# Row and padding scatters one per step, beside a new order at the start: an FNet and mixture-of-experts kernel

## The chip, the core and the metric

The kernel runs on one core of a Trainium2 chip. TensorE (PE) multiplies matrices, VectorE (DVE) and ScalarE (ACT) work on tiles, GpSimd (POOL) issues the transfers whose addresses stand in a tile of indices (gathers and scatters), and SyncE (SP) issues the plain transfers. The metric is the device time of one execution in microseconds (us), lower is better. All data are float32.

## What is computed

Eight batches of 2496 rows by 256 columns get a two-dimensional Fourier transform, of which the real part is kept. The 19968 rows that come out go through a layer of eight experts: each row goes to the one with the largest logit.

```python
X = np.fft.fft(np.fft.fft(x, axis=1), axis=2).real        # x: (8, 2496, 256)
h = X.reshape(19968, 256)
logits = h @ w_gate                                       # (19968, 8)
idx = np.argmax(logits, axis=1)
gate = softmax(logits)[row, idx]
for e in range(8):
    y[idx == e] = np.maximum(h[idx == e] @ w1[e], 0) @ w2[e]   # 256 -> 1024 -> 256
out = gate[:, None] * y
```

## The kernel before

**Mixing, per batch.** `first(b)` is stage one, in 15 steps: for each of four quarters the rows are read by SP as `xl` and, mirrored, by a POOL gather (`xh`, L233); DVE folds the two (L241 to L252); PE multiplies with a constant (`s`), ACT copies the result (L266) and SP writes it to memory (`Td`, L297). `regroup` reads it back in another order (`t<-Td`, L307). `second(b)` is stage two, in two halves: a small product `pr`, copied into place by DVE (L318), then groups of two products `p` with an ACT copy `z` between (L328), which give `rows` (L334, L335) and logits. `route` (L349 to L377) takes the largest logit, the softmax, and, by matmuls `rk` against the one-hot choice, the place of each row among those of its expert; the result is `pi`, a table of 10 row numbers per partition. Ten scatters on POOL (`Xs<-rows,pi`, helper at L177) then put the half's rows, sorted by expert, into the memory area `Xs`. `route` yields after four and after eight of them.

**Plan.** `close(b)` works out, in some 18 small DVE operations (L400 to L426), which blocks of `Xs` are now full. For the last batch it first issues 16 padding scatters (`Xs<-pad,ti`, also at L177), which fill the ends of the experts' areas.

**Experts.** The blocks come in rounds: rounds 0 and 1 have small blocks (256 and 128 rows), round 2 three blocks of 512, rounds 3 to 6 five, round 7 five and then 21 of 256. For each block SP reads its number and expert out of the plan, then the rows (`xb`, L435) and the two weight matrices (`w_sb`, L438 and L440). PE transposes the rows (`pt`, L451; DVE copies them to `xT`, L452), multiplies with the first weights (`ph`), and ACT (L491) and DVE (L489) in turn write `hT` from two PSUM buffers; then `py`, which ACT scales into `y` (L503), and one POOL scatter per 128 rows writes `out_dram<-y,ro`. `y` has two buffers.

**The order.** It is written out by hand. Stage one and two of batch 0 come first, and from the sixth step of batch 0's stage two on, one step of batch 1's stage one goes beside each step. In the main loop the work of round b-1's expert blocks has `mixed(b)` at its side: three steps of batch b+1's stage one, then steps of batch b's stage two, every other one with a step of stage one beside it, then `close(b)`. `TICKS`, 42, says how many steps of the side are spread over 0.6 of the round's work. Each engine does its instructions in the order in which the program issues them, and POOL waits for the sources of each scatter before it takes the next.

The main loop, before:

```python
        total = 16 * sum(k * size for size, k, _ in rounds()[b - 1]) / BIG
        while done < total:
            w = next(work)
            done += w
            due += TICKS * w / (0.6 * total) if w else 1
            while due >= 1:
                next(side, None)
                due -= 1
```

Of the kernel before, what the change touches and what calls it, by code (L numbers as in the profile page):

```python
# [137 lines left out]
TICKS = 42  # L138
# [18 lines left out]
def kernel(ctx: ExitStack, tc, x, w_gate, w1, w2, out):  # L157
# [57 lines left out]
    con["tri"] = bp.tile([128, 128], F32, tag="y", name="tri")  # L215
# [12 lines left out]
    def load_x(b, q):  # L228
        xl = xp.tile([NA, 4, D], F32, tag="xl", name="xl", bufs=3)
        xh = xp.tile([NA, 4, D], F32, tag="xh", name="xh", bufs=3)  # L230
        src = x[b].rearrange("(p j) d -> p j d", j=NB)
        nc.sync.dma_start(out=xl[:], in_=src[:, 4 * q + 1:4 * q + 5])
        pool.indirect_dma_start(  # L233
            out=xh[:].rearrange("p j d -> p (j d)"), out_offset=None, in_=xrows,
            in_offset=bass.IndirectOffsetOnAxis(ap=ix[:, 4 * b + q:4 * b + q + 1], axis=0))
        return xl, xh
# [41 lines left out]
    def first(b):  # L278

        x0 = ahead.pop((b, "x0"))  # L280
        pm0 = xp.tile([NA, D], F32, tag="pm0", name="pm0")
        fold_d(pm0[:], x0[:], 1)
        for q in range(5):
            f = iter(())
            if q < 4:
                xl, xh = ahead.pop((b, q))
                f = fold(xl, xh, q)
            next(f, None)
            yield
            if q:  # L290
                t1 = xp.tile([NR, 4, D], F32, tag="t1", name="t1")
                half1(b, q - 1, 0, pm, pm0, t1)
            next(f, None)
            yield
            if q:
                half1(b, q - 1, 1, pm, pm0, t1)
                nc.sync.dma_start(out=Td[b][:, 4 * (q - 1) * D:4 * q * D], in_=t1[:].rearrange("p j d -> p (j d)"))  # L297
                load(b + (q + 2) // 4, (q + 2) % 4)
            next(f, None)
            pm = xh  # L300
            yield
# [10 lines left out]
    def second(b):  # L312

        for h in range(2):
# [3 lines left out]
            vec.tensor_copy(t4[:, :, H], pr[:])  # L318
# [22 lines left out]
    def route(b, h, rows, lg):  # L341
# [37 lines left out]
        for s in range(NSL):  # L379
            sent(put_row(Xs, pi[:, s:s + 1], rows[:, s], E * CAP - 1, "xs"), b)  # L380
            if s % 4 == 3:
                yield
# [7 lines left out]
    def plan(size, k, last):  # L390
# [3 lines left out]
        def one(name, *dims, dt=F32):  # L394
# [11 lines left out]
        vec.tensor_tensor(ex[:], ce[:], nb[:], op=ALU.subtract)  # L406
        vec.scalar_tensor_tensor(rb[:], ex[:], -float(size), gone[:], op0=ALU.mult, op1=ALU.add)
# [3 lines left out]
        vec.reduce_sum(ei[:], ge[:], axis=AX_X)  # L411
        vec.tensor_tensor(eq[:], bc(ei[:], 2, E + 1), bc(bk["e9"], 1, MOST), op=ALU.is_equal)
        vec.memset(val[:, :, E:E + 1], float(E * CAP))
        vec.scalar_tensor_tensor(val[:, :, 0:E], bc(bk["i"], 2, E), float(size), bc(rb[:], 1, MOST),
                                 op0=ALU.mult, op1=ALU.add)
        vec.tensor_tensor(val[:], val[:], eq[:], op=ALU.mult)
# [11 lines left out]
        return tab  # L428
# [26 lines left out]
    def experts(todo):  # L455
# [4 lines left out]
        for k, (b, size, last, at) in enumerate(todo):  # L460
            n, m = size // 128, BIG // size
            if not k:
                got = fetch(b, size, tabs[b, size, last], at)
# [34 lines left out]
            y = bp.tile([128, BIG // 128, D], F32, tag="y", name="y")  # L498
# [12 lines left out]
    def pads(b):  # L511
# [3 lines left out]
        for e in range(E):  # L515
            for k in range(2):
                sent(put_row(Xs, ti[:, e, k:k + 1], pad[:], ROWS - 1, "xs"), b)

    def close(b):

        if b == B - 1:
            pads(b)
        for size, k, last in rounds()[b]:
            tabs[b, size, last] = plan(size, k, last)
# [7 lines left out]
    def mixed(b):  # L532
# [9 lines left out]
        close(b)  # L542
        yield from one
# [5 lines left out]
    load(0, 2)  # L549
    const("m2", "ident", "rot", "rd", "rt")  # L550
# [3 lines left out]
    vec.memset(ones[:], 1.0)  # L554

# [16 lines left out]
    early = ahead_of(1)  # L572
    for k, _ in enumerate(second(0)):
        if k > 4:
            next(early, None)
    close(0)
    work = experts(todo)
    for b in range(1, B):

        side, done, due = mixed(b), 0, 0.0  # L580
        if b == 1:
            side = chain(early, side)
        total = 16 * sum(k * size for size, k, _ in rounds()[b - 1]) / BIG
        while done < total:
            w = next(work)
            done += w
            due += TICKS * w / (0.6 * total) if w else 1
# [3 lines left out]
        for _ in side:  # L591
            pass
    for _ in work:
        pass
# [24 lines left out]
```

## Time and profile before

| what | value |
|---|---|
| median of 3 runs | 1591.04 us (1586.5 to 1600.85) |
| profiled execution | 1588.63 us, span 1586.9 us |
| granted TensorE clock, mean | 0.961 |
| PE busy | 1453.8 us, 92% of the span |
| DVE, ACT, POOL busy | 25%, 18%, 24% |

The page's first part gives the busy time of each engine. The table of stretches cuts the span and gives for each piece the busy time of the engines, the clock that PE was granted (1.00 is full speed, 2.4 GHz; 0.5 is the lower level, 1.2 GHz) and the mean busy share of the DMA engines. In the order of time a row is one instruction or several alike in a row, with start, length, engine, line, operation, tiles, and in brackets how long the engine had stood idle before it and which engine or transfer released it; "issue" means that nothing in the profile held it, "remote" that the release came from something the trace does not name.

### The profile page before, as it was taken

To read this page: it belongs to the slowest core of one execution; us is meant where nothing else is said; L and a number is where in the kernel's file an instruction comes from. 1 tells how busy PE (TensorE), PEld (TensorE's weight loads), DVE (VectorE), ACT (ScalarE), POOL (GpSimd) and SP (SyncE) were. 2 spreads that over 40 slices of the span, in tenths; PEclk is the share of its full clock that TensorE was granted. 3 is DMA by queue.
4 is the path that set the end of the run, shared out by engine and by line. 5 is a ranking of instruction groups with operands and counts; after the bars stand their busy time and mean duration, and the time that the engine had idled before them with its cause. 6 is when DMAs were issued, how large, how long until landed. Compare 5 with 4: busy or idle time off the path is not lost.

```text
span 1586.9 us, 16900 instructions
## 1 busy us (share of the span) xinstructions
PE 1453.8 (92%) x6108; PEld 1076.8 (68%) x6108; DVE 393.3 (25%) x1154; ACT 279.8 (18%) x581; POOL 373.1 (24%) x382
## 2 busy tenths in 40 slices
PE   4668897988999899989999899969999999999998
PEld 2547776765776567656677567737676688888887
DVE  2454143233144113321143111321111111111111
ACT  1222121121122112211122112201111111111111
POOL 1334215133114211331114201361111011111111
PEclk9868999998999899999999999989999999999999
DMA  7365957635234442562233432342423345545551
GB/s 195 109 205 176 302 165 218 217 95 185 92 122 158 156 150 80 164 193 85 99 119 126 176 104 87 112 159 90 149 84 117 113 137 191 188 166 175 197 188 60
DMA packets 126132, 234.20 MB, mean 148 GB/s; under 512 B 12829, under 2 KB 85648, under 8 KB 126048
## 3 DMA queue, kind: packets, MB, share of 16 engines
q1 hardware_dynamic: 103491, 178.31, 34.1%
q0 software_dynamic: 20192, 53.43, 10.0%
q10 hardware_dynamic: 2365, 1.38, 0.4%
q8 instruction: 48, 0.79, 0.2%
q14 instruction: 36, 0.29, 0.1%
HBM read 179.15 MB, written 56.28 MB: 148 GB/s over the span
## 4 chain that ended last, share of the span: by engine, by line
PE 46%; issue 31%; POOL 5%; another core or an unknown queue 3%; DVE 1%; ACT 1%; POOLq 0%; DMA 0%; ACTq 0%; DVEq 0%
PE ph L162 19%; PE py L162 18%; PE p L162 5%; POOL out_dram L177 5%; PE s L162 2%; PE pt L451 1%; POOL Xs L177 1%; POOLq L177 0%; ACT hT L491 0%; DMA Xs<-rows,pi 0%; PE rk L162 0%; DVE xT L452 0%; ACT z L328 0%; ACT rows L334 0%
## 5 line engine op out<-in xcount | busy, mean ns | idle before, releaser
L162 PE MATMUL ph<-xT,w_sb 128*128 128x512 f32 (+2 forms) x1888 | 625.1, 485 | 42.3 <-issue 21.1
L162 PE MATMUL py<-w_sb,hT 128*128 128x256 f32 x2720 | 619.7, 382 | 4.5 <-DVE hT L489 3.3
L162 PEld LDWEIGHTS py<-w_sb,hT 128*128 128x128 f32 x2720 | 515.4, 192 | 83.7 <-issue 10.3
L162 PEld LDWEIGHTS ph<-xT,w_sb 128*128 128x128 f32 x1888 | 352.8, 194 | 265.3 <-issue 208.0
L177 POOL DMA_INDIRECT out_dram<-y,ro x170 | 165.7, 974 | 980.6 <-ACT y L503 931.2
L489 DVE TENSOR_SCALAR hT<-ph 128x512 f32<-128x512 f32 x170 | 117.5, 691 | 701.1 <-issue 354.4
L503 ACT ACTIVATE y<-py,xb 128x256 f32<-128x256 f32 x170 | 80.4, 473 | 636.3 <-PE py L162 588.1
L177 POOL DMA_INDIRECT Xs<-rows,pi x160 | 160.3, 1002 | 105.0 <-issue 48.8
L491 ACT ACTIVATE hT<-ph 128x512 f32<-128x512 f32 x170 | 101.5, 597 | 413.6 <-PE ph L162 356.2
L452 DVE COPY xT<-pt 128x512 f32<-128x512 f32 (+1 forms) x87 | 59.1, 679 | 258.0 <-PE pt L451 257.6
L162 PE MATMUL p<-rd,z 128*128 128x273 f32 x320 | 95.8, 426 | 19.1 <-DVE xl L252 7.1
L162 PE MATMUL s<-xh,w 78*80 78x256 f32 (+2 forms) x272 | 82.6, 435 | 26.9 <-DVE xh L243 14.1
L162 PEld LDWEIGHTS p<-rd,z 128*128 128x128 f32 x320 | 60.5, 206 | 33.2 <-issue 13.6
L162 PEld LDWEIGHTS s<-xh,w 78*80 78x80 f32 x272 | 45.5, 176 | 48.0 <-issue 16.7
L335 DVE COPY rows<-p 128x256 f32<-128x256 f32 x80 | 34.0, 425 | 152.4 <-ACT rows L334 121.2
L162 PEld LDWEIGHTS p<-m,t 128*128 128x128 f32 x320 | 50.5, 207 | 21.0 <-issue 18.8
L233 POOL DMA_INDIRECT xh<-in_x_dram,ix x32 | 31.3, 980 | 117.6 <-PE s L162 60.2
L162 PE MATMUL p<-m,t 128*128 128x128 f32 x320 | 52.1, 292 | 0.6 <-issue 0.6
L451 PE MATMUL pt<-ident,xb 128*128 128x128 f32 x340 | 51.6, 273 | 0.0
L451 PEld LDWEIGHTS pt<-ident,xb 128*128 128x128 f32 x340 | 42.9, 142 | 8.9 <-issue 0.2
L266 ACT COPY t<-s 80x512 f32<-80x512 f32 x64 | 37.0, 581 | 57.5 <-PE s L162 50.8
L328 ACT COPY z<-p 128x256 f32<-128x256 f32 x80 | 29.8, 373 | 83.0 <-PE p L162 67.9
(79 smaller groups left out, 317.8 us busy)
## 6 DMA issues: line engine op xcount, KB each, us to landing
w_sb<-in_moe_w_dram SPq DMA_DIRECT2D x118, 1024.0 KB
xb<-Xs SPq DMA_DIRECT2D x28, 516.0 KB
Td<-t SPq DMA_DIRECT2D x32, 320.0 KB
t<-Td SPq DMA_DIRECT2D x16, 640.0 KB
xl<-in_x_dram SPq DMA_DIRECT2D x32, 312.0 KB
xb<-Xs SPq DMA_DIRECT2D x27, 258.0 KB
out_dram<-y,ro POOLq DMA_INDIRECT x170
Xs<-rows,pi POOLq DMA_INDIRECT x160
```

The source lines that it names most:

```text
L162: nc.tensor.matmul(o, lhsT=lhsT, rhs=rhs, start=start, stop=stop)
L177: return unordered(pool.indirect_dma_start(out=dst, out_offset=bass.IndirectOffsetOnAxis(ap=idx, axis=0), in_=rows, in_offset=None, bounds ...
L233: pool.indirect_dma_start(out=xh[:].rearrange("p j d -> p (j d)"), out_offset=None, in_=xrows, in_offset=bass.IndirectOffsetOnAxis(ap=ix[: ...
L266: act.copy(t1[:, 2 * half:2 * half + 2], ps[:])
L328: act.copy(z[:], p2[:])
L335: vec.tensor_copy(rows[:, k + 1, 0:D], free(p3[:], D, [-1, D]))
L451: nc.tensor.transpose(pt[:, c, t], xb[:, 2 * h + t, c * 128:(c + 1) * 128], ident[:])
L452: vec.tensor_copy(xT[:, :, 256 * h:256 * h + 128 * n], pt[:].rearrange("p c t k -> p c (t k)"))
L489: vec.tensor_scalar(o, ph[:], 0.0, None, op0=ALU.max)
L491: act.activation(o, ph[:], ACTF.Relu)
L503: act.activation(y[:, i], py[:], ACTF.Copy, scale=xb[:, i, D + 1:D + 2])
```

## The change

Row scatters and padding scatters yield after each one and not after every fourth or never; the padding is no longer in `close` but goes one scatter per step beside the expert blocks that come after the last mixing. Output tiles `y` have three buffers. The plan is a generator in five pieces, and `close` is interleaved with the other steps (`woven`). The fourth quarter of x of batch 0 is loaded with the first three, into a tile of its own tag. The copy of `pr` goes from DVE to ACT. Seven steps of batch 1's stage one come before batch 0's stage two, and then one with every other step. The steps of the side are spread over 0.7 of the round (44 steps), and experts wait for the first plan by yielding. An activation with Exp runs at the start.

```diff
-TICKS = 42
+TICKS = 44
...
-    con["tri"] = bp.tile([128, 128], F32, tag="y", name="tri")
+    con["tri"] = bp.tile([128, 128], F32, tag="xT", name="tri", bufs=1)
...
     def load_x(b, q):
-        xl = xp.tile([NA, 4, D], F32, tag="xl", name="xl", bufs=3)
-        xh = xp.tile([NA, 4, D], F32, tag="xh", name="xh", bufs=3)
+        if (b, q) == (0, 3):
+            both = bp.tile([128, 8, D], F32, tag="w1", name="x03")
+            xl, xh = both[0:NA, 0:4], both[0:NA, 4:8]
+        else:
+            xl = xp.tile([NA, 4, D], F32, tag="xl", name="xl", bufs=3)
+            xh = xp.tile([NA, 4, D], F32, tag="xh", name="xh", bufs=3)
...
-                load(b + (q + 2) // 4, (q + 2) % 4)
+                if b or q > 1:
+                    load(b + (q + 2) // 4, (q + 2) % 4)
...
-            vec.tensor_copy(t4[:, :, H], pr[:])
+            act.copy(t4[:, :, H], pr[:])
...
             sent(put_row(Xs, pi[:, s:s + 1], rows[:, s], E * CAP - 1, "xs"), b)
-            if s % 4 == 3:
-                yield
+            yield
...
-    def plan(size, k, last):
+    def plan(b, size, k, last):
...
         vec.tensor_tensor(ex[:], ce[:], nb[:], op=ALU.subtract)
+        yield
...
-        return tab
+        yield
+        tabs[b, size, last] = tab
...
             if not k:
+                while todo[0][:3] not in tabs:
+                    yield 0
                 got = fetch(b, size, tabs[b, size, last], at)
...
-            y = bp.tile([128, BIG // 128, D], F32, tag="y", name="y")
+            y = bp.tile([128, BIG // 128, D], F32, tag="y", name="y", bufs=3)
...
                 sent(put_row(Xs, ti[:, e, k:k + 1], pad[:], ROWS - 1, "xs"), b)
+                yield
+
+    def woven(*parts):
+        parts = list(parts)
+        while parts:
+            for p in list(parts):
+                if next(p, p) is p:
+                    parts.remove(p)
+                else:
+                    yield
...
-        if b == B - 1:
-            pads(b)
         for size, k, last in rounds()[b]:
-            tabs[b, size, last] = plan(size, k, last)
+            yield from plan(b, size, k, last)
...
-        close(b)
-        yield from one
+        yield from woven(close(b), one)
...
     load(0, 2)
+    load(0, 3)
...
+    warm = cp.tile([1, 1], F32, name="warm")
+    vec.memset(warm[:], 0.0)
+    act.activation(warm[:], warm[:], ACTF.Exp)
...
     early = ahead_of(1)
+    for _ in range(7):
+        next(early)
     for k, _ in enumerate(second(0)):
-        if k > 4:
+        if k % 2 == 0:
             next(early, None)
-    close(0)
...
         if b == 1:
-            side = chain(early, side)
+            side = woven(close(0), chain(early, side))
...
-            due += TICKS * w / (0.6 * total) if w else 1
+            due += TICKS * w / (0.7 * total) if w else 1
...
+    rest = pads(B - 1)
     for _ in work:
-        pass
+        next(rest, None)
```

On POOL, a regular batch (batch 5): `Xs<-rows,pi` are row scatters, `out_dram<-y,ro` output scatters, `xh` gathers of the next batch's x; x10 means ten in a row. Before, both halves:

```order
L177 DMA out_dram<-y,ro 19968x256 x2
L177 DMA Xs<-rows,pi 162048x258 x10
L233 DMA xh<-in_x_dram,ix 78x1024 x2
L177 DMA out_dram<-y,ro 19968x256 x2
L177 DMA Xs<-rows,pi 162048x258 x4
L177 DMA out_dram<-y,ro 19968x256
L177 DMA Xs<-rows,pi 162048x258 x6
L233 DMA xh<-in_x_dram,ix 78x1024
```

After, the first half:

```order
L177 DMA out_dram<-y,ro 19968x256 x2
L177 DMA Xs<-rows,pi 162048x258 x3
L237 DMA xh<-in_x_dram,ix 78x1024
L177 DMA Xs<-rows,pi 162048x258 x3
L177 DMA out_dram<-y,ro 19968x256
L177 DMA Xs<-rows,pi 162048x258 x2
L177 DMA out_dram<-y,ro 19968x256
L177 DMA Xs<-rows,pi 162048x258
L237 DMA xh<-in_x_dram,ix 78x1024
L177 DMA out_dram<-y,ro 19968x256
L177 DMA Xs<-rows,pi 162048x258
L177 DMA out_dram<-y,ro 19968x256
```

The ten row scatters of the first half, one row before, now stand in rows of 3, 3, 2, 1 and 1 with gathers and outputs between. The second half, behind the rows shown, has 1, 2, 2 and 5 with one output between each, where it had 4, an output and 6.

On POOL at the end of the last batch; `Xs<-pad,ti` are the padding scatters. Before:

```order
L177 DMA out_dram<-y,ro 19968x256 x2
L177 DMA Xs<-rows,pi 162048x258 x4
L177 DMA out_dram<-y,ro 19968x256
L177 DMA Xs<-rows,pi 162048x258 x6
L177 DMA Xs<-pad,ti 162048x258 x16
L177 DMA out_dram<-y,ro 19968x256 x75
```

After:

```order
L177 DMA Xs<-rows,pi 162048x258 x5
L177 DMA out_dram<-y,ro 19968x256 x8
L177 DMA Xs<-pad,ti 162048x258 x8
L177 DMA out_dram<-y,ro 19968x256
L177 DMA Xs<-pad,ti 162048x258
L177 DMA out_dram<-y,ro 19968x256
L177 DMA Xs<-pad,ti 162048x258
L177 DMA out_dram<-y,ro 19968x256
L177 DMA Xs<-pad,ti 162048x258
L177 DMA out_dram<-y,ro 19968x256
L177 DMA Xs<-pad,ti 162048x258 x5
L177 DMA out_dram<-y,ro 19968x256 x58
```

The sixteen padding scatters, which followed the last row scatters at once, now come behind eight more outputs, eight in a row and then singly, with a last group of five.

On PE at the start: `s` is stage one, `pr` the first product of stage two, `p` its products, with the tile that they read behind the arrow. Before, the end of batch 0's stage one and the first of its stage two:

```order
L162 MATMUL s_210<-xh,w_87 80x127
L162 MATMUL pg<-wg,rt 128x8 x4
L162 MATMUL pr<-t_222,rot 128x5
L162 MATMUL p_242<-m_88,t_222 128x128 x2
L162 MATMUL p_247<-m_88,t_222 128x128 x2
L162 MATMUL p_252<-rd,z 128x273 x2
L162 MATMUL p_258<-m_88,t_222 128x128 x2
```

After, the same place:

```order
L162 MATMUL s_212<-x_121,w_87 80x127
L162 MATMUL pg<-wg,rt 128x8 x4
L162 MATMUL s_250<-xh,w_87 80x256 x2
L162 MATMUL s_258<-xh,w_87 80x256 x2
L162 MATMUL pr<-t_224,rot 128x5
L162 MATMUL s_272<-xh,w_87 80x256 x2
L162 MATMUL p_282<-m_88,t_224 128x128 x2
L162 MATMUL p_287<-m_88,t_224 128x128 x2
L162 MATMUL p_292<-rd,z 128x273 x2
L162 MATMUL s_298<-xh,w_87 80x256 x2
L162 MATMUL p_309<-m_88,t_224 128x128 x2
```

Four matmuls of batch 1's stage one now stand ahead of `pr`, and others between it and the products of stage two; before, batch 1's first came only behind the `rk` of the first half.

## Rows read from the trace of the kernel before

**Rows 1.** Page, part 1: busy time, share of span and instruction count per engine.

```profile
PE 1453.8 (92%) x6108; PEld 1076.8 (68%) x6108; DVE 393.3 (25%) x1154; ACT 279.8 (18%) x581; POOL 373.1 (24%) x382
```

**Rows 2.** Table of stretches: from:to, length, busy time per engine, clock, DMA share, GB/s.

```profile
0.00:114.00 114.00, 61.40 (x241) 46.26 (x242) 49.48 (x174) 22.70 (x50) 34.16 (x36) 0.84 0.58 165
114.00:175.00 61.00, 52.56 (x247) 42.23 (x247) 21.64 (x85) 11.97 (x27) 26.49 (x27) 0.86 0.69 217
175.00:400.00 225.00, 196.10 (x936) 152.88 (x935) 73.90 (x241) 44.64 (x98) 65.44 (x67) 0.93 0.58 188
400.00:735.00 335.00, 318.89 (x1255) 217.33 (x1255) 88.53 (x261) 63.41 (x134) 84.10 (x87) 0.96 0.40 133
735.00:905.00 170.00, 164.58 (x659) 112.81 (x658) 46.39 (x134) 32.95 (x69) 39.36 (x41) 0.99 0.38 128
905.00:1080.00 175.00, 160.61 (x621) 107.69 (x620) 40.09 (x129) 28.77 (x62) 53.92 (x56) 0.97 0.34 117
1080.00:1580.00 500.00, 499.70 (x2159) 397.64 (x2157) 73.25 (x130) 75.18 (x141) 68.66 (x71) 1.00 0.43 147
```

**Rows 3.** Order of time, start: start, length, engine, line, instruction, idle before and releaser.

```profile
28.42 1.97 PE L162 MATMUL s<-xh,w 78*80 78x256 f32 x4 [2.06 <-issue]
...
43.25 0.56 PE L162 MATMUL pr<-t,rot 128*128 128x5 f32 x2 [8.79 <-DMA t<-Td]
...
60.75 0.17 DVE L375 TENSOR_TENSOR pi<-pf,far 128x10 int32<-128x10 f32 x1
...
62.12 0.43 PE L162 MATMUL pr<-t,rot 128*128 128x5 f32 x2
...
78.60 2.16 PE L162 MATMUL p<-rd,z 128*128 128x273 f32 x4 [6.61 <-DVE xl L252]
...
88.19 0.17 DVE L375 TENSOR_TENSOR pi<-pf,far 128x10 int32<-128x10 f32 x1
...
91.10 1.08 POOL L177 DMA_INDIRECT Xs<-rows,pi  x1 [0.30 <-issue]
...
107.22 0.38 SPq L435 DMA_DIRECT2D xb<-Xs  x1
...
107.80 0.39 SPq L438 DMA_DIRECT2D w_sb<-in_moe_w_dram  x1
...
113.76 1.53 PE L162 MATMUL ph<-xT,w_sb 128*128 128x256 f32 x6 [1.03 <-DMA w_sb<-in_moe_w_dram]
```

**Rows 4.** Order of time, padding scatters of the last batch.

```profile
1045.76 1.98 PE L162 MATMUL ph<-xT,w_sb 128*128 128x512 f32 x4 [1.38 <-issue]
...
1052.05 0.60 ACT L491 ACTIVATE hT<-ph 128x512 f32<-128x512 f32 x1 [11.43 <-remote]
...
1052.70 3.52 PE L162 MATMUL ph<-xT,w_sb 128*128 128x512 f32 x4 [4.96 <-issue]
...
1061.93 3.78 PE L162 MATMUL ph<-xT,w_sb 128*128 128x512 f32 x4 [5.71 <-issue]
```

**Rows 5.** Order of time, second half of batch 5, TensorE, ScalarE and GpSimd.

```profile
689.73 0.97 POOL L177 DMA_INDIRECT Xs<-rows,pi  x1 [1.75 <-DVE p_nb L400]
...
695.94 3.60 PE L162 MATMUL ph<-xT,w_sb 128*128 128x512 f32 x8
...
704.66 0.60 ACT L491 ACTIVATE hT<-ph 128x512 f32<-128x512 f32 x1 [3.84 <-remote]
...
705.32 5.63 PE L162 MATMUL ph<-xT,w_sb 128*128 128x512 f32 x6 [5.78 <-issue]
```

**Rows 6.** Order of time, an expert block with no mixing beside it.

```profile
1087.49 0.60 ACT L491 ACTIVATE hT<-ph 128x512 f32<-128x512 f32 x1 [2.79 <-PE ph L162]
```

**Rows 7.** Groups by line: busy, mean ns, idle before and releasers; the scatters.

```profile
L177 POOL DMA_INDIRECT out_dram<-y,ro x170 | 165.7, 974 | 980.6 <-ACT y L503 931.2 <-ACT lg L361 20.8 <-DVE ro L479 20.2
...
L177 POOL DMA_INDIRECT Xs<-rows,pi x160 | 160.3, 1002 | 105.0 <-issue 48.8 <-ACT t L266 27.6 <-ACT hT L491 10.2
...
L177 POOL DMA_INDIRECT Xs<-pad,ti x16 | 15.6, 973 | 4.9 <-issue 4.9
```

More of the change, by code (lines that the diff above doesn't have):

```diff
@@ L517, in pads @@
                 sent(put_row(Xs, ti[:, e, k:k + 1], pad[:], ROWS - 1, "xs"), b)
+                yield
+    def woven(*parts):
[5 more added lines that the diff above has]
+                else:
+                    yield
     def close(b):
-        if b == B - 1:
-            pads(b)
         for size, k, last in rounds()[b]:
-            tabs[b, size, last] = plan(size, k, last)
+            yield from plan(b, size, k, last)
     def ahead_of(b):
```

## The prediction

> **What bounds it now.** I read the profile page first, then the table of stretches, then the order of time where a stretch loses. The page [rows 1] says TensorE (PE) is busy 1453.8 of 1586.9 us. So the kernel is bound by PE, and what can be won is PE's idle time and the time that it works at a lower granted clock. The table [rows 2] says where these lie. In each row I take length minus PE busy as idle, and length times (1 - PEclk) as what the clock costs (an upper figure, since some low clock falls into idle time). The last 500 us lose 0.3 us: expert blocks alone run without a gap. The start (0 to 114) loses 52.6 us idle and 18.2 by the clock; 114 to 175 loses 8.4 and 8.5; 175 to 400, with the mixing of batches 2 and 3 beside expert blocks, 28.9 and 15.8; 400 to 735 (batches 4 and 5) 16.1 and 13.4; 735 to 905 (batch 6) 5.4 and 1.7; 905 to 1080 (batch 7 and the padding) 14.4 and 5.2. After 114 that is 73.2 us idle and at most 44.6 by the clock, about 118 in all, and it lies only where mixing runs beside experts.
>
> Why does PE wait there? In the order of time at the padding [rows 4], PE ends four `ph` matmuls at 1045.76 + 1.98 = 1047.74, but the ACT copy that only needs these starts at 1052.05, 11.43 us idle, released by "remote", and PE then stands 4.96 us. The same happens again (PE idle 5.71 before 1061.93). In a regular batch [rows 5] scatters start back to back from 689.73; PE ends `ph` at 695.94 + 3.60 = 699.54, ACT starts only at 704.66 and PE loses 5.78 us. Where no scatters run in a row the same copy starts on PE's end [rows 6]: idle 2.79, released by PE itself. So the suspect is neither ACT nor VectorE (DVE) but **the run of scatters on GpSimd (POOL)**: while POOL issues one every 1.28 us (0.97 busy and 0.30 between, [rows 7]), PE's message "done" reaches ACT and DVE up to 5 us late, `hT` is late, the two PSUM buffers of `ph` stay full, and PE stands; afterwards its clock is low for a while. The 170 output scatters, which wait for ACT (931.2 us of idle, [rows 7]), come one by one and in the last 500 us hold nothing up.
>
> **The change, part by part.** *One scatter per step.* It removes no instruction: 160 row scatters at 1002 ns, 16 padding ones at 973 and 170 output ones at 974 remain. Only the order on POOL moves. Before, a regular batch queues 10 row scatters in a row for its first half, and 4, an output, 6 and a gather for its second. After, it is 3, gather, 3, output, 2, output, 1 ... for the first, and 1, 2, 2, 5 with single outputs between for the second. What is spread by gathers and outputs that have to wait is spread in time too. But POOL does not wait for steps: outputs that are already due run at once. The row index of the second half comes about when the `py` part of a block ends, so its 10 scatters and 3 outputs may still take 13 x 1.28 = 16.6 us nearly without a break. I therefore let the first half's losses go and about half of the second's stay. Per stretch, against the idle plus clock worked out above: 400 to 735, 29.5, of which 40% = 12; 735 to 905, 7.1, of which 2; 175 to 400, 44.6, of which 12, because batch 2 keeps runs of 6 and 8 on POOL; 114 to 175, 16.9, of which 3 (that stretch is packed with transfers anyhow, DMA share 0.69). The shares are choices; their bounds are nothing, and all of it.
>
> *Padding moved behind the last plan.* Before, 16 pads follow the last 6 row scatters, and the two waits shown [rows 4] fall into them. After, the first 8 come while `ph` of the next block runs, the rest stand singly or behind outputs. Of 19.6 us I take 11. Eight in a row take 10.2 us, so a wait may remain there.
>
> *The start.* The chain [rows 3] goes: first matmul on the regrouped data (`pr`) of batch 0 at 43.25; `pi` of the first half at 60.75, 17.5 later; `pr` of the second half at 62.12, 1.4 later; `pi` of the second half at 88.19, 26.1 later, in which PE stands 6.61 for VectorE's fold of the x of batch 1, whose gather sat behind scatters, and does some 7 us of batch 1's stage one; first row scatter after that at 91.10, behind a gather; block read `xb` issued at 107.22, weights at 107.80, first `ph` at 113.76. After: x quarter 3 of batch 0 is read at the start and not after quarter 1; before, PE stood 2.06 us for it at 28.42, and the earlier read adds traffic to busy queues: between 0 and 3, I take 1.5, `pr` at 41.7. Seven steps of batch 1 fill the wait for the regrouped data, which is a wait for a transfer, so they delay nothing; `pi` at 41.7 + 17 = 58.7. The rest of stage one of batch 1 comes in the first half, where PE waited for the argmax anyway. `pr` of the second half at 60.4, and with no stage one in it and no wait on the fold 26.1 - 6.6 - 7 = 12.5 to 17 later; I take 15.8, `pi` at 76.2. No gather stands ahead, so 10 x 1.28 = 12.8 gives the last scatter ended at 89.2; `xb` some 2 later at 91.5, and the `ph` 6.5 after that (as 113.76 - 107.22) at 98. The matmuls ahead of it are the same, so 113.76 - 98 = 15.8 is won. The waits before it leave PE longer in low clock; I take off 2.8 and keep **13** (6 to 18: the lower end if the scatters still wait for a gather, the upper without the clock).
>
> *At nothing:* the copy of `pr` goes to ACT (16 small copies; ACT is busy 18% of the span [rows 1]); a third output buffer (nothing in these stretches waits for `y`; it only covers output scatters that stand behind a row scatter, 1.28 us; the last stretch has some 71 scatters in 500 us on POOL [rows 2], four to a block, so a block takes 28 us); the plan in five pieces, which delays DVE's other work less; the `tri` tile moved to a buffer not used before the first block. If cover were gone, an output scatter would be late by a run, some 10 us, and ACT would then wait for `y`. The early activation brings ACT's table load no earlier, since it still stands behind the constant loads that ACT issues. The side work now spreads over 0.7 of a round instead of 0.6; 0.3 of five 28 us blocks is 43 us before the next round needs its rows, so no fetch is late. Only round three, with three blocks, has 25, and may lose 0 to 3.
>
> **Sum.** 13 + 3 + 12 + 12 + 2 + 11 = 53. The profiled execution took 1588.6, so 1535.6; the median is 2.4 above it, so **1538** against 1591.
>
> **Rivals.** *All runs harmless.* If gaps of a few us between scatters are enough, the idle after 175 (64.8) goes whole and 13 at the start: 1591 - 78 = 1513. For it: the waits lie only in long runs. Against: the second half's 13.
>
> *Short runs harm as well.* If what counts is that POOL issues for ten or more us with or without outputs between, only the start and the padding are won: 13 + 11 = 24, so 1567. For it: [rows 5] shows the wait in a run that already had outputs in it.
>
> *POOL's runs are innocent.* Then the late "remote" releases have another cause that the change does not touch, and only the start counts: 1591 - 13 = 1578. Against it: DVE and ACT rows of the same shape lose nothing in the last 500 us, and the longest loss is where the longest run is. The Trainium skill, SBUF — State Buffer, section "Who interferes with whom", speaks for this one: DMA never contends with a compute engine, and PE and ACT never wait on anyone. By that rule spreading scatters frees nothing on PE. The trace does not agree in full: ACT waited 11.43 us for a PE that had ended [rows 4], although the port cannot be the reason; the rule covers ports, and the late signal may go another way, so I give it a small chance.
>
> *Slower.* Each scatter, alone too, holds PE's message back once, and 176 of them spread now hit 176 different handoffs instead of a few. It costs as much as is won at (118 + 13)/176 = 0.74 us each. At a scatter's own 0.98 us it is 172 - 131 = 41 slower, 1632. Against it: single output scatters in the last 500 us cost PE nothing [rows 2].
>
> **Chances.** Mine 0.54, all harmless 0.17, short runs harm 0.17, innocent 0.07, slower 0.05. The range reaches from the first to the third rival and a little over: 1512 to 1572; the likeliest case's own is 1525 to 1552. About 1% (16 us) is what a measurement of this kernel can tell: 1575 or less is faster, which the first three cases give, so 0.88; within it 0.07; slower 0.05.
>
> **What would show it.** First `ph` near 98; `pi` of batch 0's second half near 76 with no wait on the fold. Between 905 and 1080 PE idle about 6 instead of 14, and no "remote" wait of ACT over 5 us; between 400 and 735 idle near 8. POOL's rows no longer ten in a row at 1.28 us in a first half. Wrong: "remote" waits of the same length behind two or three scatters (short runs harm), or the waits gone altogether (harmless), or PE waits in the last 500 us beside single pads (slower).

## The result and the profile after

The changed kernel took 1534.05 us (median of 4 runs, 1528.0 to 1538.13), the kernel before 1595.9 (4 runs, 1586.5 to 1600.85) in the same measurement: a ratio of 0.9616, interval 0.9553 to 0.9679. On another chip it was 1527.35 against 1584.43, 0.9651 (0.9617 to 0.9684). The forecast was 1538, 53 us won; by the medians it is 61.9 here and 57.1 there.

The groups of runs went to different chips, and these are of two kinds: on two of them (and where the case was measured) the kernel before takes 1584 to 1600 us, on two others 1496 to 1497. Every ratio below is against the kernel before on the same chip. Two single runs far above the others of their kernel, 3054 us of the padding variant and 1904 us of the variant without the early read, enter no ratio.

The page of the changed kernel, part 1 (busy time, share of the span, instructions), answers to [rows 1]:

```profile
PE 1444.5 (94%) x6108; PEld 1073.5 (70%) x6108; DVE 390.3 (25%) x1139; ACT 283.7 (18%) x598; POOL 378.5 (25%) x382
```

With the spans, 1586.9 before and 1533.6 after, the 53.3 us won are 44.0 us less idle on PE (133.1 to 89.1) and 9.3 less busy time (1453.8 to 1444.5, the same matmuls at a mean clock of 0.973 and not 0.961). The table of stretches of the changed kernel answers to [rows 2]; columns as there:

```profile
0.00:114.00 114.00, 68.86 (x244) 48.71 (x244) 50.47 (x182) 23.55 (x55) 34.99 (x36) 0.85 0.61 165
114.00:175.00 61.00, 54.22 (x268) 44.82 (x268) 17.82 (x65) 12.38 (x28) 24.76 (x25) 0.89 0.77 226
175.00:400.00 225.00, 199.84 (x944) 155.89 (x945) 72.99 (x237) 46.46 (x104) 69.87 (x70) 0.95 0.58 186
400.00:735.00 335.00, 332.04 (x1326) 226.95 (x1325) 94.22 (x274) 67.91 (x144) 89.56 (x89) 0.99 0.44 142
735.00:905.00 170.00, 168.97 (x674) 115.13 (x673) 46.87 (x133) 34.55 (x73) 40.55 (x41) 1.00 0.41 136
905.00:1080.00 175.00, 173.94 (x689) 119.06 (x688) 43.02 (x133) 31.44 (x68) 40.36 (x42) 1.00 0.33 113
```

PE idle (length minus the second figure behind it), before and after: 52.6 and 45.1 in the first stretch, 8.4 and 6.8, 28.9 and 25.2, then 16.1 and 3.0, 5.4 and 1.0, 14.4 and 1.1. After 400 us nearly all the idle is gone, 30.9 of 35.9 us, and before that only 12.8 of 89.9.

Idle alone does not say what was won, since less idle can also mean slower work. A better count takes, at each border, the matmuls that are done by then, each at the time that its kind takes at full clock, and asks how far the changed kernel is ahead (an estimate from the matmul rows of both traces): 1 us at 114, 4 at 175, 10 at 400, 30 at 735, 35 at 905, 53 at 1080. On the other chip it is 1, 2, 7, 26, 33 and 52. So four fifths of the gain fall behind 400 us, and next to nothing into the start.

In the order of time of the changed kernel, the second half of batch 5 answers to [rows 5]:

```profile
702.31 7.03 PE L162 MATMUL ph<-xT,w_sb 128*128 128x512 f32 x16
...
704.28 0.60 ACT L501 ACTIVATE hT<-ph 128x512 f32<-128x512 f32 x1 [1.30 <-PE ph L162]
...
712.40 1.98 PE L162 MATMUL ph<-xT,w_sb 128*128 128x512 f32 x4 [0.93 <-issue]
713.12 0.60 ACT L501 ACTIVATE hT<-ph 128x512 f32<-128x512 f32 x1 [3.67 <-remote]
```

The late "remote" release is still there, 3.67, but PE now loses 0.93 where it lost 5.78. The start answers to [rows 3]:

```profile
24.75 1.28 ACT L575 ACT_TABLE_LOAD   x1 [24.75 <-DMA far<-c_far]
26.15 1.51 ACT L270 COPY t<-s 80x512 f32<-80x512 f32 x3
26.76 5.41 PE L162 MATMUL s<-xh,w 78*80 78x256 f32 x12 [6.58 <-ACT t L270]
...
45.49 0.59 PE L162 MATMUL pr<-t,rot 128*128 128x5 f32 x2 [0.45 <-DMA t<-Td]
...
55.64 2.01 PE L162 MATMUL p<-rd,z 128*128 128x273 f32 x8
...
67.39 0.43 PE L162 MATMUL pr<-t,rot 128*128 128x5 f32 x2
...
78.69 0.37 ACT L333 COPY z<-p 128x256 f32<-128x256 f32 x1 [3.21 <-remote]
79.11 1.12 PE L162 MATMUL p<-m,t 128*128 128x128 f32 x4 [4.21 <-issue]
...
80.03 3.32 PE L162 MATMUL p<-rd,z 128*128 128x273 f32 x8
...
87.80 0.17 DVE L380 TENSOR_TENSOR pi<-pf,far 128x10 int32<-128x10 f32 x1
...
106.46 0.21 SPq L443 DMA_DIRECT2D xb<-Xs  x1
...
115.17 5.32 PE L162 MATMUL ph<-xT,w_sb 128*128 128x256 f32 x12 [3.45 <-DVE xl L253]
```

Nothing of the forecast of the start came about as told: the first `ph` is at 115.17, not 98, and no earlier than in the kernel before (113.76). PE stands 7.5 us less there, but it has hardly done more: 244 matmuls against 241 in the first stretch, where the difference is four more of the products `p` and one `ph` less. It was busy 68.86 us for them against 61.40. Some 3 of these 7.5 us are a lower clock during the work (by the granted clock over PE's busy time an estimated 13.7 us are lost to it, against 10.4): the eight `p` at 80.03, behind a late `z`, take 3.32 us at a mean granted clock of 0.67 (80 to 84 us), the eight at 55.64 take 2.01 at 1.00 (54 to 58 us). What makes up the rest, no row settles.

### The profile page after: what moved, and what is told of

It is laid out like the page before. It is cut to its first block, busy times and chain, and to the rows that moved or that the text cites. A ratio compares the mean times of both kernels' runs of the same rounds, so it can differ in the third digit from the quotient of the medians.

```text
span 1533.6 us, 16870 instructions
## 1 busy us (share of the span) xinstructions
PE 1444.5 (94%) x6108; PEld 1073.5 (70%) x6108; DVE 390.3 (25%) x1139; ACT 283.7 (18%) x598; POOL 378.5 (25%) x382
## 4 chain that ended last, share of the span: by engine, by line
PE 49%; issue 30%; POOL 6%; DVE 1%; another core or an unknown queue 0%; POOLq 0%; ACT 0%; ACTq 0%
PE py L162 20%; PE ph L162 20%; PE p L162 5%; POOL out_dram L177 4%; PE s L162 3%; POOL Xs L177 1%; PE pt L459 1%; POOLq L177 0%; PE rk L162 0%; DVE hT L499 0%; ACT hT L501 0%; DVE xT L460 0%; PE pr L162 0%; DVE rows L340 0%
## 5 line engine op out<-in xcount | busy, mean ns | idle before, releaser
L162 PE MATMUL ph<-xT,w_sb 128*128 128x512 f32 (+2 forms) x1888 | 615.1, 479 | 18.2 <-issue 6.4
L177 POOL DMA_INDIRECT Xs<-rows,pi x160 | 165.2, 1032 | 105.8 <-issue 54.7
L162 PE MATMUL s<-xh,w 78*80 78x256 f32 (+2 forms) x262 | 78.8, 431 | 26.5 <-DVE xh L247 18.2
L237 POOL DMA_INDIRECT xh<-in_x_dram,ix x31 | 30.9, 995 | 143.8 <-PE s L162 124.9
L339 ACT COPY rows<-p 128x256 f32<-128x256 f32 x80 | 29.8, 373 | 57.9 <-PE p L162 55.5
```

The lines of the kernel that those rows point to most:

```text
L162: nc.tensor.matmul(o, lhsT=lhsT, rhs=rhs, start=start, stop=stop)
L177: return unordered(pool.indirect_dma_start(out=dst, out_offset=bass.IndirectOffsetOnAxis(ap=idx, axis=0), in_=rows, in_offset=None, bounds ...
L237: pool.indirect_dma_start(out=xh[:].rearrange("p j d -> p (j d)"), out_offset=None, in_=xrows, in_offset=bass.IndirectOffsetOnAxis(ap=ix[: ...
L339: act.copy(rows[:, k, 0:D], p3[:, 0:D])
```

## The experiments

### The two kernels on another chip

> The changed kernel itself again, since the kernel before took 1496 us in the four comparisons made first and 1591 when the case was measured. Two theories. One: the late messages belong to the chip or its hour, not to the program; where the kernel before takes 1496 the scatters have nothing to give, only the start is won, and the ratio is 0.993 to 0.995; where it takes 1591 the ratio is 0.96 again. Two: the late messages belong to the program and something in the three variants happened to remove them; then the ratio is near 0.96 wherever it runs.

Measured: 0.9651 (0.9617 to 0.9684), the kernel before at 1584.43. On such a chip both theories give this ratio, so it does not decide between them. What does is that the kernel before itself takes 1496 us in some comparisons and 1584 or 1600 in others, and that two variants that had 0.994 and 0.995 on a chip at 1496 have 0.967 and 0.965 on one at 1600 (below). So the late messages come with the chip, or with the hour at which it was used: each chip was seen in one comparison only.

> The kernel before, for a trace from the same chip as the others of this call. If the late messages belong to the chip, PE idle between 400 and 1080 is either about 36 us (time near 1591) or under 5 (time near 1496), with the same runs of ten scatters at 1.28 us in both.

Measured: 1579.52, PE idle after 400 like that of [rows 2]:

```profile
400.00:735.00 335.00, 319.48 (x1253) 215.29 (x1252) 89.88 (x264) 65.02 (x136) 84.47 (x85) 0.97 0.42 140
735.00:905.00 170.00, 164.74 (x660) 113.06 (x659) 46.20 (x134) 32.83 (x69) 40.09 (x41) 0.99 0.37 126
905.00:1080.00 175.00, 160.87 (x624) 108.28 (x623) 39.38 (x128) 28.77 (x62) 54.52 (x56) 0.95 0.33 114
```

15.5, 5.3 and 14.1: 34.9 us, in the same runs of scatters.

### A run of scatters by itself

```diff
+            kind, count = PROBE.get(len(todo) - k, ("", 0))
+            for r in range(count):
+                if kind == "plain":
+                    nc.sync.dma_start(out=Jk2[128 * r:128 * r + 128], in_=pad[:])
+                    continue
+                put_row(Junk, (jt if kind == "put" else jo)[:, ...], pad[:], ..., "junk")
```

> The changed kernel with extra transfers at the start of six of the last blocks, where nothing else is mixed in: runs of 4, 8 and 12 scatters to a memory area that nobody reads, 12 scatters whose row numbers are all out of range (issued, nothing moved), 12 plain writes of the same size issued by SP, and 8 scatters again. If a run of scatters on POOL holds PE's messages back, PE waits none or little at 4, 1 to 3 us at 8, 5 or more at 12, and at the 12 that move nothing as well if it is the issuing, not if it is the data; none at the plain writes. If the runs are innocent, PE waits nowhere. On a chip on which the kernel before takes 1496 I expect no wait at any of them.

Measured, on the chip of the two runs above, as PE idle in gaps over 0.5 us between the first scatter of a run and 6 us after its last:

| put at the start of a block | in a row | PE idle |
|---|---|---|
| scatters | 4 | 0 |
| scatters | 8 | 0.76, and 0 the second time |
| scatters | 12 | 1.45 and 2.27 |
| scatters with all rows out of range | 12 | 2.18 |
| plain writes by SP | 12 | 0 |

The run of 12 scatters, in order of time:

```profile
1324.75 0.60 PE L459 MATMUL pt<-ident,xb 128*128 128x128 f32 x4
...
1329.50 0.69 DVE L460 COPY xT<-pt 128x512 f32<-128x512 f32 x1 [7.32 <-PE py L162]
...
1330.25 3.72 PE L162 MATMUL ph<-xT,w_sb 128*128 128x256 f32 x16 [1.45 <-DVE xT L460]
...
1336.24 3.72 PE L162 MATMUL ph<-xT,w_sb 128*128 128x256 f32 x16 [2.27 <-ACT hT L513]
```

The transposes `pt` end at 1325.35; the copy that needs them, and for which the rows show nothing else to wait for, starts at 1329.50, 4.15 later. Around the 12 that move nothing it is the same (`jo` is their table of rows):

```profile
1391.49 0.69 DVE L460 COPY xT<-pt 128x512 f32<-128x512 f32 x1 [8.05 <-issue]
1391.95 0.97 POOL L177 DMA_INDIRECT Junk<-pad,jo  x1 [0.30 <-issue]
...
1392.24 2.23 PE L162 MATMUL ph<-xT,w_sb 128*128 128x256 f32 x7 [2.18 <-DVE xT L460]
```

So on this chip it is POOL's run itself that delays PE's messages, with no mixing and no plan beside it; not the data moved, and not a transfer of that size as such. This is one execution, with one run of each kind and two of eight. In it the wait begins at about eight in a row and is smaller than I had put it (3.7 us for twelve, not five or more).

### Many short runs

```diff
                 put_row(out, ro[:, i:i + 1], y[:, i], NT - 1, "out")
+                for _ in range(2 if last else 0):
+                    put_row(Junk, jt[:, spent[0]:spent[0] + 1], pad[:], 96 * 128 - 1, "junk")
+                    spent[0] += 1
```

> The changed kernel with 84 extra scatters to an area that nobody reads, two behind each output scatter of the last 21 blocks, so never more than three in a row. The rival by which each scatter holds PE back once, 0.74 us or more, makes it 60 us slower than the changed kernel. By the prediction's own theory, three in a row cost nothing: the same within 3 us.

Measured, on the same chip: 1524.43 (1523.09 to 1525.78) against the changed kernel's 1527.35. 84 more scatters in runs of three cost nothing. The rival that ends slower, 0.74 us each, would have been 62 us slower; it is excluded for scatters in threes beside expert blocks.

### Row scatters ten in a row again

```diff
         for s in range(NSL):
-            sent(put_row(Xs, pi[:, s:s + 1], rows[:, s], E * CAP - 1, "xs"), b)
+            for r in range(4 * s, min(4 * s + 4, NSL)):
+                sent(put_row(Xs, pi[:, r:r + 1], rows[:, r], E * CAP - 1, "xs"), b)
             yield
```

All ten steps stay; only the scatters move together, into the order that the kernel before has on POOL.

> The changed kernel with the row scatters in three steps again (4, 4 and 2), all ten steps of each half kept, so that only their place on GpSimd's queue moves: ten in a row in a first half, four, an output and six in a second. Theory of the prediction (a run of scatters holds back PE's messages): the idle of PE between 400 and 905, 4.0 us in the changed kernel, goes back to some 15 to 21, the remote waits of ACT and DVE return, and the time is 20 to 30 us above the changed kernel, about 1560. If only long runs in the phase of the first expert product cost anything, and the second halves now fall mostly elsewhere: 8 to 15 above. If the runs are innocent: no difference, 1534.

Measured: 1486.78, ratio 0.9944 (0.9924 to 0.9964), the kernel before at 1496.19 on that chip. The 1560 that I expected were for a chip of the first kind, and this is one of the other. The table of stretches from 400 to 1080 shows it:

```profile
400.00:735.00 335.00, 334.97 (x1354) 231.42 (x1353) 94.14 (x268) 69.43 (x148) 88.02 (x88) 1.00 0.44 142
735.00:905.00 170.00, 169.99 (x694) 118.36 (x693) 43.36 (x126) 35.13 (x75) 41.84 (x42) 1.00 0.39 129
905.00:1080.00 175.00, 174.99 (x678) 118.69 (x677) 41.44 (x128) 30.56 (x64) 57.36 (x59) 1.00 0.38 127
```

0.05 us idle in 680, with runs of 10 to 13 at 1.28 us on POOL as in the kernel before. Here the runs are innocent. The same kernel again:

> The changed kernel with the row scatters in three steps again (4, 4, 2), as in the first comparison of this kind, which fell on a chip where the kernel before takes 1496 us. On a chip where it takes some 1585 the changed kernel took 0.9651 of it. If ten in a row are what holds PE's messages back there, PE idle between 400 and 905 goes from 2.1 us to some 15 to 20 and the ratio to 0.98; if only the place of the runs against the expert blocks counts, and that is little moved here, the ratio is 0.970. If the start and the plan brought the gain, it stays at 0.965. On a chip where the kernel before takes 1496 the ratio is 0.994 again.

Measured: 1548.7, ratio 0.9666 (0.9627 to 0.9706), the kernel before at 1600.4: a chip with late messages, and yet hardly worse than the changed kernel's 0.9616 and 0.9651, where I expected 0.98. Its table from 400 to 1080:

```profile
400.00:735.00 335.00, 326.41 (x1306) 223.66 (x1307) 94.10 (x274) 66.76 (x142) 87.83 (x89) 0.99 0.44 142
735.00:905.00 170.00, 166.97 (x659) 112.94 (x658) 46.20 (x132) 33.45 (x71) 40.71 (x41) 0.98 0.38 128
905.00:1080.00 175.00, 171.92 (x665) 115.92 (x664) 40.92 (x128) 31.40 (x68) 40.83 (x42) 0.99 0.35 120
```

8.6, 3.0 and 3.1 us idle: 14.7, between the 5.1 of the changed kernel and the 35.9 of the kernel before. By run of scatters, batches 4 to 7 (PE idle in gaps over 0.2 us between its first scatter and 6 us after its last):

| run | kernel before | ten in a row, ten steps | changed kernel |
|---|---|---|---|
| first half | 2.60, 2.41, 1.01, 0 | 0, 0, 0, 0 | 0, 0, 0, 0 |
| second half | 5.33, 5.78, 4.39, (see padding) | 3.04, 2.66, 2.95, 3.06 | 1.01, 0.93, 0.93, 1.05 |

A first half has the same ten scatters at 1.28 us in the kernel before and here, beside `ph` in both, and loses nothing here. What differs is what else PE does in the run. In the kernel before, at the end of batch 5's first run (649.49 to 664.73):

```profile
662.23 1.88 PE L162 MATMUL ph<-xT,w_sb 128*128 128x512 f32 x4
...
663.94 0.61 PE L162 MATMUL p<-m,t 128*128 128x128 f32 x4
666.53 0.37 ACT L328 COPY z<-p 128x256 f32<-128x256 f32 x1 [2.26 <-remote]
...
666.96 2.19 PE L162 MATMUL p<-rd,z 128*128 128x273 f32 x4 [2.41 <-ACT z L328]
```

and here, in the run from 637.78 to 652.6:

```profile
644.02 7.03 PE L162 MATMUL ph<-xT,w_sb 128*128 128x512 f32 x16
```

Before, a half's scatters take three steps, so the second half's stage two, in which PE waits for `z` after every `p`, begins while POOL is still in the run. With ten steps it begins behind the run: in this run's PE rows stands no `p`, only `ph`, `py` and a few `s`. So the yields do more than part the scatters: they hold the following steps off. That this is why the loss went is read from the rows, and not tested by itself (the third output buffer, the ACT copy and the plan in pieces are in this kernel too); batch 7's first half in the kernel before had `p` and `z` beside eleven in a row too, without stage one, and lost nothing.

### Padding in front of the last plan again

```diff
+        if b == B - 1:
+            for _ in pads(b):
+                pass
         for size, k, last in rounds()[b]:
             yield from plan(b, size, k, last)
```

> The changed kernel with the sixteen padding scatters back in front of the last plan, in one row behind the last row scatters. If the run holds PE back, 14 us of idle between 905 and 1080 return in part: PE idle there 8 to 12 instead of 1.1, the time 10 to 16 us above the changed kernel, 1544 to 1550. If runs are innocent: no difference.

Measured: 1487.15, ratio 0.9948 (0.993 to 0.9965), the kernel before at 1496.19: the chip on which runs cost nothing, PE idle 0.01 between 905 and 1080.

> The changed kernel with the sixteen padding scatters in front of the last plan. Where the kernel before takes some 1585: PE idle between 905 and 1080 goes from 0.1 us to 8 to 12, the ratio from 0.965 to 0.972 or 0.975. If the padding cost nothing there: 0.965. Where it takes 1496: 0.995 again.

Measured: 1542.85, ratio 0.9649 (0.9615 to 0.9682), the kernel before at 1600.4. The time cannot tell it from the changed kernel; the order of time can, where 16 padding scatters run from 1036.10 to 1056.3:

```profile
1046.07 3.62 PE L162 MATMUL py<-w_sb,hT 128*128 128x256 f32 x16
...
1054.70 0.47 ACT L513 ACTIVATE y<-py,xb 128x256 f32<-128x256 f32 x1 [12.29 <-remote]
1055.22 5.67 PE L162 MATMUL py<-w_sb,hT 128*128 128x256 f32 x16 [5.54 <-issue]
```

5.54 and, behind it, 0.90 us: 6.4 in this run, against none in the changed kernel and 14.25 in the kernel before, where row scatters and padding made one run of 27 with one output in it. The second half's run before it lost 1.02 here; together that is less idle than the 8 to 12 that I expected. So with the padding in its old place, in front of the last plan, about half of the 14.25 us is gone all the same: the one run has become two, with 4 us between them, but the other parts of the change are in this kernel too, and no run tells which of them it was. Nearly all the rest goes with the padding's new place: 1.05 stay in the changed kernel.

### The scatters alone, on the kernel before

The edit is that of `route`, `pads` and `TICKS` in the diff of the change, nothing else.

> The kernel before with the scatters alone changed: row scatters one per step, padding scatters behind the last mixing one per step, the side's steps spread over 0.7 of a round with 44. Start, plan, buffers and copies as before. If the scatters carry the gain, the stretches after 400 us get all that the changed kernel shows (PE idle 16.1 + 5.4 + 14.4 = 35.9 down to about 5) with the low clock behind it, some 40 us: 1551 to 1556, and what is left to the changed kernel, some 15 us, is the start's. If the start and the interleaved plan carry more, the time lies above 1565.

Measured: 1501.03, ratio 1.0039 (1.0025 to 1.0053). On this chip there is nothing for it to gain; it loses 5 us.

> The kernel before with the scatters alone changed (row scatters one per step, with the ten steps that this gives each half, padding behind the last mixing, side steps over 0.7 of a round), start, plan, output buffers and copies as before. On the chip where the kernel before takes 1496 it took 1501. The run with the rows in three steps but all ten steps kept had ratio 0.967 on a chip where the kernel before takes 1600, so single scatters alone are worth little. If the steps put between runs, which move stage one's transfers away from the scatters, carry the rest, then PE idle between 400 and 1080, 34.9 us in the kernel before, is 3 to 6 here and the ratio is 0.975 to 0.98 (all but the start). If the third output buffer, the ACT copy or the plan in pieces carry it, idle there stays above 15 and the ratio above 0.985. Where the kernel before takes 1496: 1.004 again.

Measured: 1501.22, ratio 1.0035 (1.0019 to 1.0052), again a chip on which the kernel before takes 1496. So the question of this run, how much of the gain after 400 us these edits bring without the buffer, the copy and the plan, stays open. What the first run does show is the rest of the change: 14 us lie between it and the two variants above, 1501.03 against 1486.78 and 1487.15, on the same chip. By the count of matmuls done, the variants are 7 and 9 us ahead of it at 400 us, and 12 and 14 at 1080. Of the 5 us that are added behind 905, 3.1 are idle time of PE in this kernel (171.90 us busy of 175). The first `ph` is at 109.42 and 108.29 in them, at 114.83 here.

### The fourth quarter of x loaded late again

```diff
-                if b or q > 1:
-                    load(b + (q + 2) // 4, (q + 2) % 4)
+                load(b + (q + 2) // 4, (q + 2) % 4)
...
-    load(0, 3)
```

> The changed kernel with one part undone: the fourth quarter of x of batch 0 is loaded after the first quarter of stage one again. In the changed kernel's trace the first ACT copy of stage one came at 26.15 us instead of 20.32, behind constant loads that ACT issues and that paused from 13.2 to 21.7, and PE stood 6.58 instead of 1.48 us there. If the earlier read of 0.6 MB is what holds ACT's loads up, that wait falls back to about 1.5, the wait of 2.06 for the fourth quarter returns, and the first half's row numbers come some 3 us earlier: 0.998 of the changed kernel's time, some 1531 us, PE idle before 60 us about 3 less. If instead the new activation with its table load is the cause, the 6.6 us stay and the return of the wait costs 1 to 2 us: 1536.

Measured: 1485.22, ratio 0.9935 (0.9912 to 0.9958). The order of time, against the start of the changed kernel above:

```profile
20.09 1.28 ACT L569 ACT_TABLE_LOAD   x1 [20.09 <-DMA cap<-c_cap]
...
21.49 1.51 ACT L266 COPY t<-s 80x512 f32<-80x512 f32 x3
...
22.10 2.42 PE L162 MATMUL s<-xh,w 78*80 78x256 f32 x5 [1.80 <-ACT t L266]
```

The activation with its table load is still there, and ACT's first copy is back at 21.49 from 26.15: the earlier read held ACT's constant loads up, not the activation. All traces agree on this: the copy starts at 23.85 to 26.85 in the eight with the early read and at 20.32 to 22.33 in the six without. PE gets the 2.06 us wait for the quarter back (2.19 here). At `pr`, further on, little is left of it: 43.89 here against 46.31 and 45.14 in the two variants on this chip, but 45.29 when this kernel ran again, and 43.21 to 46.31 over all eight traces with the early read. So the early read wins nothing there, and a loss of 1 to 2 us is not shown.

> The changed kernel with the fourth quarter of x of batch 0 loaded after the first quarter again. Where the kernel before takes 1496 its ratio was 0.9935, the lowest of the four there by a hair, the wait for ACT's first copies 1.8 instead of 6.4 to 7.1 us and a wait of 2.2 for the quarter back. Where the kernel before takes some 1585 to 1600: the same 2 to 4 us at the start, ratio 0.961 to 0.964 against 0.962 to 0.965 of the changed kernel, first expert matmul at 108 to 112 instead of 112 to 115.

Measured: 1485.87, ratio 0.9929 (0.99 to 0.9958), on a chip of the other kind once more. In time it can't be told from the variants that keep the early read, 0.9944 and 0.9948. It has the lowest times of all kernels here, but by less than the intervals.

## Why the prediction was right, point by point

**The bound and the cause: right, for this kind of chip.** PE waits for late messages while POOL runs through scatters: the probe shows it with no mixing beside. One reading was too strong: the 11.43 us before ACT's copy [rows 4] are its whole idle time, of which 4.3 lie behind the end of PE's matmuls (1047.74 to 1052.05). What the prediction couldn't see from one trace is that the delay depends on the chip, or on its state at that hour: on two of the chips the same runs at the same 1.28 us cost nothing, and the gain there is 0.5 to 0.7% (variants of the changed kernel; it was not run there itself), not 3.5 to 3.8%.

**The rule against it.** The Trainium skill, SBUF — State Buffer, section "Who interferes with whom", says that DMA never contends with a compute engine and that PE and ACT never wait on anyone. On the two chips at 1496 the traces agree (0.05 us idle in 680 beside full runs). On the others engines do wait: ACT started 12.29 us after its last work, and 5.01 us after PE had ended, beside the 16 padding scatters. The 12 scatters that move nothing delay it too, so it does not look like a matter of ports, though no run shows the way that the message takes. The rule about ports is not contradicted, but it was no ground for the rival "POOL's runs are innocent", which would have given 1578.

**The stretches after 400 us: too small.** Forecast 12 + 2 + 11 = 25; the idle alone fell by 13.1 + 4.4 + 13.3 = 30.8, and with the clock at 0.99 to 1.00 the lead grew by 20 + 6 + 18, from 10 to 53 us. The step that failed is "about half of the second's stay": 0.93 to 1.05 us stay of 4.4 to 5.8. I took the change to act by breaking the runs, and the second half's 13 transfers in 16.6 us are in fact hardly broken. The run with ten in a row shows why it went further: with the ten steps kept, the first halves lose nothing and the second halves only about half, ten in a row or not. Between 400 and 905 us PE's idle is 21.5 in the kernel before, 11.6 with ten in a row and ten steps, 4.0 in the changed kernel. Only the last 7.6 of this are the shorter runs (some 2 us for each second half), on which the prediction built. The 9.9 before them came with the scatters in a row as before; the rows point at the steps that hold the next work off, and no run separates these from the rest of the change.

**The start: too large.** Forecast 13, and at 114 us the changed kernel is 1 us ahead. Three terms were off. The earlier x read was put at a gain of 1.5, `pr` at 41.7; it came at 45.49, and the read brought nothing, since it delays ACT's constant loads (shown by the run without it). "`pr` of the second half at 60.4" was 67.39, also because stage one's matmuls that stand ahead of it (61.77 to 67.39) do not fit into the wait for the argmax, where I had put them. And its 15.8 us took 20.4, with a late release of 3.21 in it [the row at 78.69], at the end of the first half's scatters, which run here in a row too: 6, a gather and 4, and I had priced their delay in the later stretches only. On the chips without late messages that way takes 13.8 to 14.5 us (in the padding variant `pr` at 67.02, `pi` at 80.86), and there the start does win: the first `ph` is at 106.22 to 109.42 in the four traces of variants with the new start, at 114.83 and 112.89 in the two with the old one. On the others it is at 112.09 to 115.17 with the new and at 113.76 and 114.11 with the old.

**114 to 400: too large.** Forecast 3 + 12; idle fell by 1.6 + 3.7. From 175 to 400 the clock rose from 0.93 to 0.95, some 4 us, and the lead grew by 3 + 6. What stays is waits of `rk` for the argmax (2.57 and 2.23 us, on both kinds of chip) and long runs of batches 2 and 3.

**The sum.** 53 was forecast, and the two profiled executions differ by 53.3: up to 400 us the forecast was 28 and 10 came, behind it 25 and 43. The total was right by terms that were wrong in both directions, and that is luck; the mechanism was right, its sizes were not.

**The rivals.** "All runs harmless" was right behind 400 us in outcome and wrong before. "Short runs harm" has two sides. That two or three in a row would do harm is excluded by four in a row (0) and by 84 scatters in threes (no slower). That ten or more us of issuing do the same harm with outputs between is answered by the changed kernel: its second halves issue for 16.6 us with outputs between and lose 0.93 to 1.05 us, not 4.4 to 5.8. "Slower" is excluded by the 84 as well.

**Open.** Why the chips differ, no run tells. One more difference goes with it. Part 6 of a page gives, where it can, the median time from a transfer's issue to its landing. The row scatters, in the changed kernel where it was measured and in the variant with rows in three steps at 1496:

```profile
Xs<-rows,pi POOLq DMA_INDIRECT x160
...
Xs<-rows,pi POOLq DMA_INDIRECT x160, 5.0
```

All six traces from the chips at 1496 have this time (4.8 to 5.1 us) and no idle that is put down to "remote"; the eight others have no time, since three to four tenths of the completion records of POOL's transfers are missing in them, and 11 to 22 "remote" waits each. So what delays the messages may also lose records, or the recording may have a part in the delay; every time here comes from an execution with a recorded span and clock, so no run tells these apart. Nor was it separated, on a chip with late messages, how much of the gain comes from the ten steps alone and how much from the third output buffer, the plan in pieces or the ACT copy: both runs of the scatters alone fell on the other kind.

## What to carry to other kernels

When an engine starts late on a release whose sender has long ended, look at what POOL issues at that time: a run of eight or more indirect transfers may hold the release back (in the probe four did not, twelve cost 3.7 us). Breaking the run helped here, and the rows suggest that letting only long products with few handoffs stand beside it helps as well. Judge a stretch by the work done at its end, not by its idle time. And compare a kernel on more than one chip before a wait of this kind is called the kernel's own.

## What was not expected of the hardware

The same program has different times on different chips (each seen in one comparison), 1496 against 1584 to 1600 us for the kernel before, with POOL's scatters at the same 0.97 us and 0.30 between, and, after 400 us, with no idle of PE on the one kind beside runs after which it waits on the other. Scatters that move nothing delay PE's messages like those that do: 2.18 us of idle for 12 of them. And a read of 0.6 MB issued by SP and POOL at the start holds up constant loads issued by ACT: ACT's copy that stands behind them came at 23.85 to 26.85 us, and at 20.32 to 22.33 without the read.
